# The small room moved to last but one, the last visit's tiles written one behind the other, weight buffers counted by use

## The chip, the core and the metric

One NeuronCore of a Trainium2 chip runs the whole kernel. The metric is the device time of one execution in microseconds, as the median of several runs. Engines: TensorE (PE, matmuls), VectorE (DVE), ScalarE (ACT), GpSimd (POOL, here the issuer of gathers and scatters) and SyncE (SP, which issues the weight loads).

## The reference

```python
# attention: q, k, v are (8, 8, 576, 64); mask 0 <= i - j < 128, bias -slope[h] * |i - j|
attn = softmax(where(mask, q @ k.T / 8 + bias, -1e9)) ; x = attn @ v        # -> (8, 576, 512)
# mixture of experts, 8 experts, w1 (8, 512, 1024), w2 (8, 1024, 512)
logits = x @ w_gate ; local = sigmoid(x @ w_local)
for s in range(576):                      # per batch
    e = argmax(logits[s]) if s == 0 or local[s] < 0.5 else prev_e ; prev_e = e
    out[s] = softmax(logits[s])[e] * (relu(x[s] @ w1[e]) @ w2[e])
```

All of it is in 32-bit floats.

## The kernel before, in words

The first part (attention and routing) fills about the first 280 us and is not touched. It leaves the tokens x in DRAM, grouped in blocks of 32, and tables of indices.

The second part is a list of **visits**, `PLAN`. A visit takes one expert's weights and a number of rows gathered for it. Three visits belong to fixed experts; the others go by rank, that is by how many tokens an expert got, and their sizes stand in `RANKS`. `ORDER_OF_ROOMS` puts them in order. By rows the rank visits run 512, 288, 384, 416, 256, 288, 384, 192, 256, 384, 224, 32. The text calls the 384-row visit near the end the long 384-row visit, and the one of 32 rows the small room.

A visit (`Fixed.run`) loops over eight hidden blocks f of 128. For each, 12 matmuls (`three`, once for each of 4 pieces of 128) make the hidden block h in PSUM; ScalarE writes its positive part hh (a reduced 32-bit type) and VectorE the rest hl; then `second(f - 1)` multiplies the block before with the second layer, three matmuls of 512 columns for each output tile of 128 rows. Every 32-bit product is made of three: high by high, high by low, low by high. A visit of 256 rows has two output tiles, ys[0] and ys[1]. `finish` scales an output tile, on ScalarE for even and on VectorE for odd tiles, and `scatter` sends it to the output through GpSimd.

**Weights** come through `Stream`, here W. A chunk (2 hidden blocks of one layer, "a" or "b", 512 KB) is loaded by SP into one of six raw buffers (`wraw`), then split: two casts on ScalarE for the high part, two subtractions on VectorE for the low part, into one of six `cut` buffers. `load` may run `RAWS` chunks ahead of the last one split, `fill` splits up to six chunks ahead of the first one in use. The small room's chunks are used raw, and its first-layer chunks lie in other buffers (`xT`).

**Rows** come through `Feed`. At each `tick` inside a visit it issues a gather (`take`, `gate`) on GpSimd and may `turn` a gathered tile: a transpose on VectorE into the single buffer xtr, a cast on ScalarE and a subtraction on VectorE, which write the high and low part of the tile qx that the h matmuls read. `turn` takes only tiles of visits up to `upto`, the next one; `Feed.finish` turns what is left at a visit's end.

The small room (`Mini`) comes last. Its first layer is put between the last h block and `second(7)` of the visit ahead of it, its hidden layer is turned by PE inside `second(7)`, and its second layer follows. After all visits the waiting scatters are issued, and a loop for tokens left over runs no times.

Of the kernel before, what the change touches and what calls it, by code (L numbers as in the profile page):

```python
# [16 lines left out]
P = 128  # L17
# [3 lines left out]
DM = 512  # L21
# [4 lines left out]
OWN = [2, 3, 4]  # L26

RANKS = [(512, 288), (384, 256), (384, 256), (384, 224), (416,), (288,), (192,), (32,)]
ORDER_OF_ROOMS = [0, 1, 2, 8, 3, 9, 4, 10, 5, 6, 7, 11]
NSB = 128  # L30
NFX = 32
SB = S // 32
# [48 lines left out]
def moe_attention(ctx, tc, qT, kT_d, vv, wg, wl, w1, w2, out):  # L81
# [65 lines left out]
    def run(g):  # L147
        for _ in g:
            pass
# [96 lines left out]
    class Stream:  # L246


        def __init__(self, order):
            self.order = order  # L250
            self.raw, self.cut, self.gone, self.n_raw, self.n_cut, self.first, self.depth = [], {}, set(), 0, 0, 0, 1

        def load(self):
            while self.n_raw < len(self.order) and self.n_raw < self.n_cut + RAWS:
                e, which, c, kind = self.order[self.n_raw]
                if kind and which == ("b" if kind == "also" else "a"):
                    if c % 2 == 0:
                        self.pair = tp.tile([P, 2, 2, DM], F32, name="xT")
                    t = self.pair[:, c % 2]
                else:  # L260
                    t = wr.tile([P, 2, DM], F32, name="wraw")
                self.raw.append(load_chunk(e() if callable(e) else e, which, c, t))
                self.n_raw += 1

        def fill(self):
            while self.n_cut < len(self.order) and self.n_cut < self.first + self.depth:
                self.load()
                if self.order[self.n_cut][3] == "only":
                    self.cut[self.n_cut] = self.raw.pop(0)
                    self.n_cut += 1  # L270
                else:
                    run(self.split(self.room(), now.act, nc.vector))
            self.load()

        def room(self):
            pool = vp if (self.n_cut - 1) % SPLITS < 4 else wp
            return pool.tile([P, 2, 2, DM], F32R, name="cut")

        def split(self, c, scalar, vector):
            raw = self.raw.pop(0)  # L280
            self.cut[self.n_cut] = c[:, 0], c[:, 1], raw
            self.n_cut += 1
            yield from split_chunk(raw, c, scalar, vector, self.n_cut - 1 if self is W else 0)

        def find(self, which):
            return min(i for i in self.cut if self.order[i][1] == which)

        def at(self, which):
            self.depth = min(self.depth + 1, SPLITS)
            self.fill()  # L290
            return self.cut[self.find(which)]

        def done(self, which):
            i = self.find(which)
            del self.cut[i]
            self.gone.add(i)
            while self.first in self.gone:
                self.first += 1
            self.fill()
# [717 lines left out]
    class Fixed:  # L1017
        def __init__(self, rows):
            self.rows = rows

        def run(self, W, tick, mini=None, ready=None):
            N = 32 * self.rows.blocks
            wins = windows(self.rows.blocks)
            n, rest = len(wins), wins[-1][1] % 4
            M = N - 32 * rest
            ys = [py.tile([P, DM], F32, name="y")[:, :P * r] for _, r in wins]
            xh, xl = self.rows.xh[:, :, :N], self.rows.xl[:, :, :N]
            hs, hx = {}, None

            def second(f, then=()):  # L1030
                hh, hl = hs.pop(f)
                vh, vl, raw = W.at("b")
                for t, (w, r) in enumerate(wins):
                    if r == 4:
                        sl = slice(32 * w, 32 * w + P)
                        three(ys[t], hh[:, sl], hl[:, sl], vh[:, f % 2], vl[:, f % 2], f == 0, f == 7)
                    elif f % 2:
                        rests(ys[t], lambda ff: hx[:, ff % 2], raw, (f - 1, f), r)
                    if t == n // 2 - 1:
                        tick()  # L1040
                        for g in then:
                            g()
                if f % 2:
                    W.done("b")

            for f in range(8):
                ah, al, _ = W.at("a")
                hp = ph_.tile([P, N], F32, name="h")
                for kc in range(4):
                    cs = slice(P * kc, P * kc + P)  # L1050
                    three(hp, ah[:, f % 2, cs], al[:, f % 2, cs], xh[:, kc], xl[:, kc], kc == 0, kc == 3)
                    if kc == 1:
# [12 lines left out]
                tick()  # L1065
                if f > 0:
                    second(f - 1)
                if rest and f % 2:
                    hx = hx_next
                tick()  # L1070
            if mini:
                ready()
                mini.first(W)
            second(7, [mini.turn] if mini else ())
            for t in range(n):
                c = self.rows.t0 + t
                finish(ys[t], self.rows.g[:, t:t + 1], self.rows.idx[2][:, c:c + 1], t % 2)
# [8 lines left out]
    class Mini(Fixed):  # L1086


        def first(self, W):
            raws = [W.at("a") if i == 0 else W.cut[W.find("a") + i] for i in range(4)]  # L1090
            hp = ph_.tile([P, 256], F32, name="h")
            for kc in range(4):
                for g in range(4):
# [190 lines left out]
    now.act = act  # L1284
    for i, v in enumerate(visits):
        if isinstance(v, Fixed):
            mini = visits[i + 1] if i + 2 == len(visits) else None
            v.run(W, lambda: feed.tick(i + 1), mini, lambda: feed.finish(i + 1))
            feed.finish(i + 1)
    assert table_done  # L1290

# [55 lines left out]
```

## Time and profile before

| | |
|---|---|
| median of 3 runs | 679.7 us (679.34 to 679.98) |
| the profiled execution | 678.48 us, of which its span is 676.8 us |
| PE busy | 656.5 us, 97% of the span |
| VectorE, ScalarE, GpSimd busy | 69%, 62%, 58% |
| mean granted TensorE clock | 0.995 |
| moved by DMA | 121 MB, mean 179 GB/s |

The span is the time from the first to the last instruction of the profiled execution. A busy share is a mean over the whole span; what bounds a stretch is read from the windows and the timeline of that stretch. Matmul durations overlap: a matmul counts as busy until its result is out, while the next one has already begun, so the start-to-start distance is what a matmul costs.

### The profile page before, as it was taken

To read this page: it belongs to the slowest core of one execution; us is meant where nothing else is said; L and a number is where in the kernel's file an instruction comes from. 1 tells how busy PE (TensorE), PEld (TensorE's weight loads), DVE (VectorE), ACT (ScalarE), POOL (GpSimd) and SP (SyncE) were. 2 spreads that over 40 slices of the span, in tenths; PEclk is the share of its full clock that TensorE was granted. 3 is DMA by queue.
4 is the path that set the end of the run, shared out by engine and by line. 5 is a ranking of instruction groups with operands and counts; after the bars stand their busy time and mean duration, and the time that the engine had idled before them with its cause. 6 is when DMAs were issued, how large, how long until landed. Compare 5 with 4: busy or idle time off the path is not lost. (4 is left out here: it accounts for less than half of the span.)

```text
span 676.8 us, 16362 instructions
## 1 busy us (share of the span) xinstructions
PE 656.5 (97%) x5485; PEld 528.0 (78%) x5485; DVE 466.0 (69%) x1637; ACT 418.1 (62%) x1217; POOL 392.6 (58%) x655
## 2 busy tenths in 40 slices
PE   8999999999999989999999999999999999999993
PEld 4667777677666678878888888988898898899882
DVE  6579889889888999975553657453776547774520
ACT  7999999999989644343442555353665536653421
POOL 7856656556687745877775476471577516761011
PEclk9999999999999999999999999999999999999998
DMA  9855754764813675554654268343846834774810
GB/s 287 275 143 156 240 170 144 218 194 152 255 68 110 196 265 179 164 148 148 228 189 135 82 225 281 96 133 128 287 152 205 281 99 143 241 224 152 274 54 34
DMA packets 60903, 121.09 MB, mean 179 GB/s; under 512 B 9260, under 2 KB 28204, under 8 KB 60816
## 3 DMA queue, kind: packets, MB, share of 16 engines
q1 hardware_dynamic: 51248, 100.12, 46.5%
q0 software_dynamic: 9136, 19.30, 9.3%
q8 instruction: 44, 0.72, 0.4%
q10 hardware_dynamic: 432, 0.59, 0.3%
q14 instruction: 43, 0.35, 0.2%
HBM read 101.03 MB, written 19.29 MB: 178 GB/s over the span
## 5 line engine op out<-in xcount | busy, mean ns | idle before, releaser
L182 POOL DMA_INDIRECT kr<-xd,xidx x141 | 155.3, 1101 | 55.3 <-issue 39.4
L1004 PE MATMUL h<-qx,cut 128*128 128x384 f32 (+6 forms) x440 | 142.4, 324 | 0.0
L1005 PE MATMUL h<-qx,cut 128*128 128x384 f32 (+6 forms) x440 | 140.8, 320 | 0.2 <-DVE qx L192 0.2
L1006 PE MATMUL h<-qx,cut 128*128 128x384 f32 (+6 forms) x440 | 140.9, 320 | 0.0
L243 DVE TENSOR_TENSOR cut<-wraw,cut 128x512 fp32r<-128x512 f32 x183 | 118.8, 687 | 30.0 <-ACT cut L241 28.6
L1056 ACT ACTIVATE hh<-h 128x384 fp32r<-128x384 f32 (+4 forms) x104 | 46.6, 448 | 132.9 <-PE h L1006 131.2
L167 POOL TENSOR_SCALAR cut<-cut,r 128x192 f32<-128x192 f32 (+2 forms) x256 | 99.6, 407 | 45.8 <-DVE r L167 16.2
L998 POOL DMA_INDIRECT out<-y,sidx x41 | 44.5, 1085 | 132.7 <-ACT y L1013 85.3
L1057 DVE SCALAR_TENSOR_TENSOR hl<-h,hh 128x256 fp32r<-128x256 f32 (+4 forms) x112 | 55.4, 496 | 88.4 <-ACT hh L1056 88.0
L1004 PE MATMUL y<-cut,hh 128*128 128x512 f32 x288 | 113.7, 395 | 0.8 <-ACT hh L167 0.8
L1006 PE MATMUL y<-cut,hl 128*128 128x512 f32 x288 | 113.1, 394 | 0.9 <-DVE hl L1057 0.9
L1005 PE MATMUL y<-cut,hh 128*128 128x512 f32 x288 | 113.3, 393 | 0.0
L167 ACT ACTIVATE cut<-scs,mn 128x192 f32<-128x192 f32 (+2 forms) x256 | 108.8, 429 | 5.3 <-DVE mn L167 5.0
L241 ACT CAST cut<-wraw 128x512 fp32r<-128x512 f32 x164 | 93.6, 618 | 24.6 <-PE y L1006 23.9
L1004 PEld LDWEIGHTS h<-qx,cut 128*128 128x128 f32 x440 | 83.0, 189 | 9.7 <-issue 3.9
L167 DVE CUSTOM_DVE_ANT_0 scs<-sc,bias 128x192 f32<-128x192 f32 (+2 forms) x288 | 83.1, 324 | 8.9 <-PE sc L167 5.6
L1005 PEld LDWEIGHTS h<-qx,cut 128*128 128x128 f32 x440 | 83.1, 189 | 5.7 <-DVE qx L192 0.7
L1006 PEld LDWEIGHTS h<-qx,cut 128*128 128x128 f32 x440 | 83.2, 189 | 2.7 <-issue 0.2
L167 PE MATMUL pt<-ident,cut 128*128 128x128 f32 x448 | 70.8, 282 | 0.6
L1006 PEld LDWEIGHTS y<-cut,hl 128*128 128x128 f32 x288 | 54.0, 188 | 13.5 <-DVE hl L1057 2.1
L167 PE MATMUL sc<-kr,qx 64*64 64x192 f32 (+2 forms) x1152 | 61.9, 319 | 1.2 <-DVE mn L167 1.2
L1004 PEld LDWEIGHTS y<-cut,hh 128*128 128x128 f32 x288 | 54.2, 188 | 10.7 <-ACT hh L167 1.8
(218 smaller groups left out, 1036.7 us busy)
## 6 DMA issues: line engine op xcount, KB each, us to landing
wraw<-w SPq DMA_DIRECT2D x100, 512.0 KB
xT<-w SPq DMA_DIRECT2D x20, 512.0 KB
kr<-kT SPq DMA_DIRECT2D x31, 288.0 KB
qx<-qT SPq DMA_DIRECT2D x30, 288.0 KB
cut<-v SPq DMA_DIRECT2D x8, 1024.0 KB
xd<-T SPq DMA_DIRECT2D x8, 768.0 KB
xd<-T SPq DMA_DIRECT2D x8, 384.0 KB
kr<-xd,xidx POOLq DMA_INDIRECT x141, 3.8
```

Source lines behind the costliest of these rows:

```text
L167: ins = getattr(self.engine, name)(*args, **kw)
L182: queued(nc.gpsimd.indirect_dma_start(out=r, out_offset=None, in_=src[0:n, :], in_offset=bass.IndirectOffsetOnAxis(ap=col, axis=0), bounds ...
L241: scalar.copy(c[:, 0, f], raw[:, f])
L243: (pool if 2 * n + f == POOL_CUT else vector).tensor_tensor(c[:, 1, f], raw[:, f], c[:, 0, f], ALU.subtract)
L998: queued(nc.gpsimd.indirect_dma_start(out=out.rearrange("t (a c) -> (t a) c", a=n), out_offset=bass.IndirectOffsetOnAxis(ap=col, axis=0), ...
L1004: nc.tensor.matmul(o, ah, bh, start=start, stop=False)
L1005: nc.tensor.matmul(o, ah, bl, start=False, stop=False)
L1006: nc.tensor.matmul(o, al, bh, start=False, stop=stop)
L1056: now.act.activation(hh, hp[:, :M], AF.Relu)
L1057: nc.vector.scalar_tensor_tensor(hl, hp[:, :M], 0.0, hh, ALU.max, ALU.subtract)
```

## The change

The rank visits now run 512, 288, 384, 416, 256, 288, 384, 192, 384, 224, 32, 256: the small room is last but one, and the 256-row visit that stood between the 192-row and the long 384-row one is last. The small room still shares its first layer and turn with the 224-row visit. In the last visit (`tail`) the second layer of blocks 5 to 7 is put off for output tile 1 and done as a whole behind tile 0; each tile is finished and scattered as soon as it is complete; scatters still waiting are issued ahead of the visit. `Stream` counts raw buffers by use: a raw buffer is live from its load until its chunk is split (or, for a chunk used raw, until it is done with), at most `RAWS` are live, chunks that lie in other buffers don't count but wait for their turn, and `fill` splits only what an earlier call has loaded, unless the chunk is asked for. The buffer for a split is chosen by a counter of splits.

```diff
-ORDER_OF_ROOMS = [0, 1, 2, 8, 3, 9, 4, 10, 5, 6, 7, 11]
+ORDER_OF_ROOMS = [0, 1, 2, 8, 3, 9, 4, 10, 6, 7, 11, 5]
...
+        def paired(self, i):
+            _, which, _, kind = self.order[i]
+            return kind in ("also", "only") and which == ("b" if kind == "also" else "a")
         def load(self):
-            while self.n_raw < len(self.order) and self.n_raw < self.n_cut + RAWS:
+            while self.n_raw < len(self.order) and self.live < RAWS:
                 e, which, c, kind = self.order[self.n_raw]
-                if kind and which == ("b" if kind == "also" else "a"):
+                if self.paired(self.n_raw):
+                    if self.n_raw > self.first + 2 * SPLITS:
+                        return
...
                     t = wr.tile([P, 2, DM], F32, name="wraw")
+                    self.live += 1
...
-        def fill(self):
-            while self.n_cut < len(self.order) and self.n_cut < self.first + self.depth:
+        def fill(self, upto=-1):
+            while self.n_cut <= upto or self.n_cut < min(self.first + self.depth, self.ready):
                 self.load()
...
             self.load()
+            self.ready = self.n_raw
         def room(self):
-            pool = vp if (self.n_cut - 1) % SPLITS < 4 else wp
-            return pool.tile([P, 2, 2, DM], F32R, name="cut")
+            self.n_room += 1
+            return (vp if (self.n_room - 1) % SPLITS < 4 else wp).tile([P, 2, 2, DM], F32R, name="cut")
         def split(self, c, scalar, vector):
             raw = self.raw.pop(0)
             self.cut[self.n_cut] = c[:, 0], c[:, 1], raw
+            if not self.paired(self.n_cut):
+                self.live -= 1
...
         def done(self, which):
             i = self.find(which)
             del self.cut[i]
             self.gone.add(i)
+            if self.order[i][3] in ("only", "raw") and not self.paired(i):
+                self.live -= 1
...
-        def run(self, W, tick, mini=None, ready=None):
+        def run(self, W, tick, mini=None, ready=None, tail=False):
...
-                if f > 0:
+                if tail and f == 6:
+                    vh, vl, _ = W.at("b")
+                    hh, hl = hs[5]
+                    three(ys[0], hh[:, 0:P], hl[:, 0:P], vh[:, 1], vl[:, 1], False, False)
+                elif f > 0 and not (tail and f == 7):
                     second(f - 1)
...
+            if tail:
+                assert n == 2 and not rest
+                chunks = [W.at("b"), W.at("b", 1)]
+                for t, fs in ((0, (6, 7)), (1, (5, 6, 7))):
+                    for f in fs:
+                        hh, hl = hs[f]
+                        sl, (vh, vl, _) = slice(P * t, P * t + P), chunks[f // 2 - 2]
+                        three(ys[t], hh[:, sl], hl[:, sl], vh[:, f % 2], vl[:, f % 2], False, f == 7)
+                    c = self.rows.t0 + t
+                    finish(ys[t], self.rows.g[:, t:t + 1], self.rows.idx[2][:, c:c + 1], t)
+                    scatter(*pending.pop())
...
-            mini = visits[i + 1] if i + 2 == len(visits) else None
-            v.run(W, lambda: feed.tick(i + 1), mini, lambda: feed.finish(i + 1))
+            mini = visits[i + 1] if i + 1 < len(visits) and isinstance(visits[i + 1], Mini) else None
+            if i + 1 == len(visits):
+                while pending:
+                    scatter(*pending.pop(0))
+            v.run(W, lambda: feed.tick(i + 1), mini, lambda: feed.finish(i + 1), i + 1 == len(visits))
```

What it moves, at the places of which the prediction speaks. First VectorE in the 192-row visit, before: y is an output tile of the visit ahead, xtr, kr and qx are a tile being turned for the next visit, cut a split chunk, hl the low part of a hidden block.

```order
L1011 TENSOR_SCALAR y_8816<-y_8499,gs_7991 128x512
L188 STREAM_TRANSPOSE xtr_8830<-kr_8513 128x512
L243 TENSOR_TENSOR cut_8807<-xT_8632,cut_8807 128x512 x2
L192 TENSOR_TENSOR qx_8829<-xtr_8830,qx_8829 128x4x128
L1057 SCALAR_TENSOR_TENSOR hl_8848<-h_8822,hh_8847 128x128
L188 STREAM_TRANSPOSE xtr_8853<-kr_8513 128x512
L192 TENSOR_TENSOR qx_8829<-xtr_8853,qx_8829 128x4x128
L1057 SCALAR_TENSOR_TENSOR hl_8883<-h_8863,hh_8882 128x128
```

The same place after the change:

```order
L1027 TENSOR_SCALAR y_8843<-y_8502,gs_8008 128x512
L188 STREAM_TRANSPOSE xtr_8857<-kr_8516 128x512
L243 TENSOR_TENSOR cut_8836<-xT_8563,cut_8836 128x512 x2
L192 TENSOR_TENSOR qx_8856<-xtr_8857,qx_8856 128x4x128
L1073 SCALAR_TENSOR_TENSOR hl_8875<-h_8849,hh_8874 128x128
L188 STREAM_TRANSPOSE xtr_8880<-kr_8516 128x512
L192 TENSOR_TENSOR qx_8856<-xtr_8880,qx_8856 128x4x128
L188 STREAM_TRANSPOSE xtr_8887<-kr_8516 128x512
L192 TENSOR_TENSOR qx_8856<-xtr_8887,qx_8856 128x4x128
L1073 SCALAR_TENSOR_TENSOR hl_8914<-h_8894,hh_8913 128x128
```

A third transpose and subtraction stand between the second tile and the low part of the second hidden block.

VectorE after the change, from the end of the 224-row visit (hl_9685 is its last hidden block, y_9740 its second output tile) to the first hidden blocks of the last visit (hl_9839 and hl_9856):

```order
L1073 SCALAR_TENSOR_TENSOR hl_9685<-h_9671,hh_9684 128x224
L243 TENSOR_TENSOR cut_9785<-wraw_9751,cut_9785 128x512 x2
L1027 TENSOR_SCALAR y_9740<-y_9458,gs_8947 128x512
L243 TENSOR_TENSOR cut_9798<-wraw_9758,cut_9798 128x512 x2
L188 STREAM_TRANSPOSE xtr_9806<-kr_9468 128x512
L192 TENSOR_TENSOR qx_9805<-xtr_9806,qx_9805 128x4x128
L188 STREAM_TRANSPOSE xtr_9810<-kr_9468 128x512
L192 TENSOR_TENSOR qx_9805<-xtr_9810,qx_9805 128x4x128
L1073 SCALAR_TENSOR_TENSOR hl_9839<-h_9825,hh_9838 128x256
L1073 SCALAR_TENSOR_TENSOR hl_9856<-h_9842,hh_9855 128x256
```

Both tiles of the last visit are turned there, behind the 224-row visit's output and a split; before, nothing followed that output.

GpSimd's queue at the end, before (y_9980 and y_9982 are the two tiles of the 224-row visit, y_10017 is the small room's):

```order
L998 DMA out<-y_9737,sidx_111 4608x512
L998 DMA out<-y_9739,sidx_111 4608x512
L998 DMA out<-y_9980,sidx_111 4608x512
L998 DMA out<-y_9982,sidx_111 4608x512
L998 DMA out<-y_10017,sidx_111 18432x128
```

And after the change, where y_9738, y_9740 and y_9803 are these three, y_10010 and y_10024 the tiles of the last visit:

```order
L1014 DMA out<-y_9455,sidx_111 4608x512
L182 DMA gs_9556<-gd_76,ridx_110 128x1
L1014 DMA out<-y_9738,sidx_111 4608x512
L1014 DMA out<-y_9740,sidx_111 4608x512
L1014 DMA out<-y_9803,sidx_111 18432x128
L1014 DMA out<-y_10010,sidx_111 4608x512
L1014 DMA out<-y_10024,sidx_111 4608x512
```

Two scatters follow the last visit instead of three that follow the small room and its neighbour.

## Rows read from the trace of the kernel before

**Rows 1.** The page: busy time, share of the span and instructions of PE, and the granted TensorE clock by fortieths of the span in tenths of full speed.

```profile
PE 656.5 (97%) x5485; PEld 528.0 (78%) x5485; DVE 466.0 (69%) x1637; ACT 418.1 (62%) x1217; POOL 392.6 (58%) x655
PEclk9999999999999999999999999999999999999998
```

**Rows 2.** The windows from 480 to 660 us, nine of 20 us: the line with their sum, busy us of each engine.

```profile
sum 180.00, PE 179.98 PEld 158.66 DVE 108.83 ACT 91.44 POOL 84.96; mean PE 20.00 PEld 17.63 DVE 12.09 ACT 10.16 POOL 9.44
```

**Rows 3.** The timeline of the end: start, duration in us, engine, line, operation, output and inputs, form, count; in brackets the idle time before and what ended it.

```profile
662.35 0.69 ACT L1013 ACTIVATE y<-y,gs 128x512 f32<-128x512 f32 x1 [0.48 <-PE y L1006]
...
662.83 0.40 PE L1006 MATMUL y<-cut,hl 128*128 128x512 f32 x1
...
663.26 0.75 DVE L1011 TENSOR_SCALAR y<-y,gs 128x512 f32<-128x512 f32 x1 [4.29 <-PE y L1006]
663.31 0.98 POOL L998 DMA_INDIRECT out<-y,sidx  x1 [14.54 <-ACT hh L1106]
...
663.35 1.96 PE L1084 MATMUL y<-wraw,hh 128*32 128x128 f32 x64
665.37 0.37 ACT L1013 ACTIVATE y<-y,gs 128x128 f32<-128x128 f32 x1 [2.08 <-PE y L1084]
667.23 0.98 POOL L998 DMA_INDIRECT out<-y,sidx  x1 [2.94 <-issue]
670.60 0.98 POOL L998 DMA_INDIRECT out<-y,sidx  x1 [2.39 <-issue]
```

**Rows 4.** The view of line 998, the scatters: under what their engine waited for, the landing of a scatter (us in total, times); then the time from issue to landing of all 41.

```profile
  DMA out<-y,sidx: 8.6, 3
...
DMA to landing us min/median/max: 2.8/4.0/6.7
```

**Rows 5.** The timeline of PE in the 256-row visit: its first matmul, the second and the 24th, then the first and the last of ten matmuls in a row of its second layer, then the first of the next visit.

```profile
582.89 0.39 PE L1004 MATMUL h<-qx,cut 128*128 128x256 f32 x1
583.11 0.28 PE L1005 MATMUL h<-qx,cut 128*128 128x256 f32 x1
...
585.75 0.28 PE L1006 MATMUL h<-qx,cut 128*128 128x256 f32 x1
...
603.25 0.39 PE L1006 MATMUL y<-cut,hl 128*128 128x512 f32 x1
...
605.31 0.39 PE L1006 MATMUL y<-cut,hl 128*128 128x512 f32 x1
605.53 0.33 PE L1004 MATMUL h<-qx,cut 128*128 128x384 f32 x1
```

**Rows 6.** The timeline of the 224-row visit: a split (casts on ScalarE, subtractions on VectorE), and two steps of the visit without one.

```profile
645.95 1.14 ACT L241 CAST cut<-wraw 128x512 fp32r<-128x512 f32 x2 [1.04 <-PE y L1006]
...
646.61 1.29 DVE L243 TENSOR_TENSOR cut<-wraw,cut 128x512 fp32r<-128x512 f32 x2 [1.27 <-ACT cut L241]
...
652.74 0.36 ACT L1056 ACTIVATE hh<-h 128x224 fp32r<-128x224 f32 x1 [2.37 <-PE h L1006]
...
655.46 0.36 ACT L1056 ACTIVATE hh<-h 128x224 fp32r<-128x224 f32 x1 [2.37 <-PE h L1006]
```

**Rows 7.** The last weight load's issue in SP's timeline, and the DMA view of 641 to 647 us: the busy share of the 16 DMA engines in tenths, by fortieths of the window (0.15 us each). The second burst, from the 24th digit on, belongs to the scatter at 643.32.

```profile
641.14 0.33 SPq L236 DMA_DIRECT2D wraw<-w  x1
...
DMA  5444322949337989597646000289992000000000
```

**Rows 8.** The timeline of GpSimd: the last gather ahead of a long idle stretch and the scatter that ends it; then two scatters of output tiles of the long 384-row visit.

```profile
543.66 0.99 POOL L182 DMA_INDIRECT kr<-xd,xidx  x1 [0.31 <-issue]
561.14 1.02 POOL L998 DMA_INDIRECT out<-y,sidx  x1 [16.48 <-ACT y L1013]
...
638.76 0.98 POOL L998 DMA_INDIRECT out<-y,sidx  x1 [23.52 <-ACT y L1013]
643.32 0.99 POOL L998 DMA_INDIRECT out<-y,sidx  x1 [3.58 <-DVE hl L1057]
```

**Rows 9.** The timeline of the 192-row visit: the turn of the second tile (transpose, cast, subtraction), the low part of the second hidden block, and the matmul that reads it.

```profile
564.61 0.70 DVE L188 STREAM_TRANSPOSE xtr<-kr 128x512 f32<-128x512 f32 x1
565.35 0.62 ACT L191 CAST qx<-xtr 128x512 fp32r<-128x512 f32 x1 [0.39 <-DVE xtr L188]
566.00 0.69 DVE L192 TENSOR_TENSOR qx<-xtr,qx 128x512 fp32r<-128x512 f32 x1 [0.69 <-ACT qx L191]
566.61 0.28 DVE L1057 SCALAR_TENSOR_TENSOR hl<-h,hh 128x128 fp32r<-128x128 f32 x1
566.95 0.49 PE L1006 MATMUL y<-cut,hl 128*128 128x512 f32 x1
```

**Rows 10.** Windows of the end: from and to, length, then for each engine busy us and instructions; behind them the mean granted clock, the DMA share and GB/s.

```profile
670.00:670.50 0.50, 0.00 (x0) 0.00 (x0) 0.00 (x0) 0.00 (x0) 0.00 (x0) 0.89 0.00 0
670.50:671.00 0.50, 0.00 (x0) 0.00 (x0) 0.00 (x0) 0.00 (x0) 0.40 (x1) 0.50 0.00 0
```

**Rows 11.** The timeline of PE at the start of the kernel: two groups of warm-up matmuls.

```profile
1.06 3.59 PE L167 MATMUL pk<-warm 128*128 128x512 f16 x8 [1.06 <-DVE warm L167]
...
9.35 1.47 PE L167 MATMUL pk<-warm 128*128 128x512 f16 x6
```

**Rows 12.** The waits of PE in the whole trace: us in total, times, longest.

```profile
PE h L1005 <- DVE qx L192: 0.2, 1, 0.2
```

More of the change, by code (lines that the diff above doesn't have):

```diff
@@ L250, in __init__ @@
             self.order = order
-            self.raw, self.cut, self.gone, self.n_raw, self.n_cut, self.first, self.depth = [], {}, set(), 0, 0, 0, 1
+            self.raw, self.cut, self.gone = [], {}, set()
+            self.n_raw = self.n_cut = self.n_room = self.first = self.live = self.ready = 0
+            self.depth = 1
+        def paired(self, i):
+            _, which, _, kind = self.order[i]
+            return kind in ("also", "only") and which == ("b" if kind == "also" else "a")
         def load(self):
-            while self.n_raw < len(self.order) and self.n_raw < self.n_cut + RAWS:
+            while self.n_raw < len(self.order) and self.live < RAWS:
                 e, which, c, kind = self.order[self.n_raw]
-                if kind and which == ("b" if kind == "also" else "a"):
+                if self.paired(self.n_raw):
+                    if self.n_raw > self.first + 2 * SPLITS:
+                        return
                     if c % 2 == 0:
@@ L261, in load @@
                     t = wr.tile([P, 2, DM], F32, name="wraw")
+                    self.live += 1
                 self.raw.append(load_chunk(e() if callable(e) else e, which, c, t))
                 self.n_raw += 1
-        def fill(self):
-            while self.n_cut < len(self.order) and self.n_cut < self.first + self.depth:
+        def fill(self, upto=-1):
+            while self.n_cut <= upto or self.n_cut < min(self.first + self.depth, self.ready):
                 self.load()
-                if self.order[self.n_cut][3] == "only":
+                if self.order[self.n_cut][3] in ("only", "raw"):
                     self.cut[self.n_cut] = self.raw.pop(0)
@@ L281, in split, with find, at @@
             self.cut[self.n_cut] = c[:, 0], c[:, 1], raw
+            if not self.paired(self.n_cut):
+                self.live -= 1
             self.n_cut += 1
             yield from split_chunk(raw, c, scalar, vector, self.n_cut - 1 if self is W else 0)
-        def find(self, which):
-            return min(i for i in self.cut if self.order[i][1] == which)
-        def at(self, which):
+        def find(self, which, nth=0):
+            return [i for i in range(self.first, len(self.order)) if self.order[i][1] == which and i not in self.gone][nth]
+        def at(self, which, nth=0):
             self.depth = min(self.depth + 1, SPLITS)
-            self.fill()
-            return self.cut[self.find(which)]
+            i = self.find(which, nth)
+            self.fill(i)
+            return self.cut[i]
         def done(self, which):
@@ L1070, in run @@
                 tick()
+            if tail:
[9 more added lines that the diff above has]
+                    scatter(*pending.pop())
+                W.done("b")
+                W.done("b")
+                return
             if mini:
@@ L1089, in first @@
         def first(self, W):
-            raws = [W.at("a") if i == 0 else W.cut[W.find("a") + i] for i in range(4)]
+            raws = [W.at("a", i) for i in range(4)]
             hp = ph_.tile([P, 256], F32, name="h")
```

## The prediction

> **What bounds the kernel now.** I began with the page [rows 1]: TensorE (PE) is busy 656.5 of 676.8 us, and its granted clock is at full speed in every slice but the last. Then the windows of the late visits [rows 2]: from 480 to 660 us PE is busy 179.98 of 180.00. So until the last matmul the time is a count of matmuls, and a wait put in front of PE there is added in full, since nothing later has room to take it back. Last the timeline of the end [rows 3]: the last matmul ends at 665.31, the span at 676.80. These 11.49 us belong to GpSimd's queue: three scatters at 663.31, 667.23 and 670.60, though their data is ready at 663.04, 664.01 and 665.74. Scatters wait for one another: the view of their line names the landing of an earlier one as what later ones waited for, and a landing takes 2.8 to 6.7 us [rows 4]. From the last scatter's start to the end it is 6.20 us.
>
> I keep the old trace's clock: the 256-row visit (582.89 to 605.53 [rows 5]) is cut out and put behind 665.31.
>
> **The move itself.** The visit took 22.64 us. Its 96 matmuls of 256 columns are 0.12 us apart (23 of them from 583.11 to 585.75), its 48 of 512 columns 0.229 (ten from 603.25 to 605.31 [rows 5]): 22.5 us. In its old place it also covered the turning of three tiles for the next visit; at the end it covers none. Term: -0.1 us. The small room's matmuls, its wait for the copied hidden layer and its scatter stay.
>
> **Weight buffers.** The order of loads, splits and matmuls is unchanged until the 192-row visit, so I cost the new counting up to there at nothing. In the 224-row visit five chunks of the last visit are now split: ten casts and ten subtractions of some 0.6 us each, in gaps of ScalarE of 2.37 us per step of 2.72 [rows 6]; VectorE's gaps are alike. The small room's four second-layer chunks hold four of the six raw buffers until its matmuls end, so these loads go in turn through the other two, each issued when a split frees its buffer. A pair of subtractions ends 1.95 us behind its first cast (645.95 to 647.90 [rows 6]), so two steps less 1.95 leave 3.5 us from that to the split that wants the new chunk. A load alone, issued at 641.14, has stopped moving data by some 644.3, 3.1 us later [rows 7]. It fits with 0.4 us to spare, and a late cast has 1.2 us more before the next activation waits behind it. Cost: nothing. If the cover fails it comes back at the last visit's start, below.
>
> **Gathers.** The long 384-row visit now follows the 192-row one, so its 12 row gathers and 3 gates run where 8 and 2 ran, before 560 us: five more at 1.3 us, in an idle stretch of GpSimd of 16.48 us [rows 8]. Nothing.
>
> **The third tile in the 192-row visit.** Before, this visit turned two tiles for its successor; now three. In VectorE's order the third transpose and subtraction stand ahead of the low part hl of the second hidden block. On the old clock the second subtraction ends at 566.69; then a transpose of 0.70, a cast of 0.62 and a subtraction of 0.69, one behind the other because they share one buffer, with 0.03 to 0.06 us between them, end at 568.83 [rows 9]. hl starts near 568.75 instead of 566.61. The matmul that reads it started at 566.95, right behind hl's end at 566.89, and would start at 569.09. Term: +2.1 us. Bounds: 0 if it is absorbed, 2.5 if the cast waits a little for ScalarE.
>
> **The start of the last visit.** Its tiles are turned only after the small room's code, since the feed turns tiles for a visit that is next and no further. In VectorE's order: the 224-row visit's second output tile, a split of two subtractions, then transpose, subtraction, transpose, subtraction. The split's casts stand behind the small room's copy on ScalarE, and their target buffer is free when the 224-row visit's last matmul ends, 662.83 + 0.40 = 663.23 [rows 3]: casts from 663.28, the split done 1.95 later, 665.23. A turn is transpose, cast, subtraction: 2.08 us from start to end (564.61 to 566.69 [rows 9]). So the first ends at 667.3. The second starts behind it, has its cast done at 668.7 and ends at 669.4. PE is free at about 665.1, since a matmul's modelled tail overlaps the next by some 0.2 us (0.28 busy, 0.12 apart [rows 5]). Its first two matmuls need both casts; the third needs the low parts, and 21 follow closely. Delay: 669.4 - 665.1 - 0.24 of work = 4.1 us. Bounds: 2.9 if the split were done before (the first transpose then starts at 664.0); 5.2 if a load is 1.1 us late.
>
> **The tail.** Tile 0 of the last visit now ends nine matmuls ahead, 9 x 0.229 = 2.06 us. With E the end of the last matmul: its ScalarE output takes 0.05 + 0.69 us and the scatter follows 0.27 later, as 663.04 to 663.31 [rows 3]: E - 1.05. The second scatter waits for that landing: 3.92 us between the first pair of rows 3, 3.37 between the next, and 4.56 where loads run beside them [rows 8]. I take 3.92, a pair of full-width tiles as here: E + 2.87. Then 6.20 us, and 0.5 more (estimated: a full tile's data moves longer than the small room's): E + 9.57, against E + 11.49. With 3.37 it is E + 9.0. Between them the term is -2.1 us. Bounds: -1.3 (4.56), and -4.0 if the scatter waits only for its data at E + 0.8.
>
> **Sum.** -0.1 + 2.1 + 4.1 - 2.1 = +4.0 us on the profiled execution: 678.48 becomes 682.5. The median of the runs, 679.7, lies 1.2 above that execution, so I forecast **683.7 us**, 0.6% slower. About 0.2%, 1.4 us, is what a measurement here can tell from no change.
>
> **Rivals.**
>
> *The clock falls in the gap* (0.13). PE would stand 3.6 us, issue two matmuls, and stand 0.5 more. After the last matmul the granted clock stayed at 1.00 until about 670.4, when PE had stood 5.1 us, then read 0.50 [rows 10]: from 2.4 to 1.2 GHz. For it: the gap is not much shorter. Against: it is shorter. Price: the eight warm-up matmuls that open the kernel took 3.59 us; six later ones took 1.47, so eight at full speed would take 1.47 + 2 x 0.229 = 1.93 [rows 11, 5]. A slow restart of that size costs 1.7 us: 685.4.
> The Trainium skill, "TensorE: Matmul & The Clock Gate", section "HAM oscillation — how this bites in real kernels", has a stream of matmuls that is broken by waits throttled again in the wait and each group started cold. By that rule the time would be the 685.4 of this rival. The trace agrees only that the clock falls after work stops; no gap inside this kernel is long enough to show more.
>
> *The third tile is absorbed* (0.12): 683.7 - 2.1 = 681.6. For: the 256-row visit covered three turns and lost 0.1 us [rows 5]. Against: there hidden blocks lay between the tiles; here none does.
>
> *Every turn is covered, the tail alone counts* (0.05). Place: the tile turns ahead of PE. In the whole trace PE waited once on a turned tile, 0.2 us [rows 12]. If the last visit's turn ended before PE is through with the small room, the 4.1 and 2.1 us would go and the 2.1 of the tail stay gained: 677.5, faster. It decides by whether the last turn's end, which I put at 669.4, comes before 665.1; the split and both turns would have to start 4.3 us earlier than the order of instructions lets them.
>
> *The edit does less than it says* (0.02): the tail's pair of scatters 4.56 us apart and a load 1.1 us late: 683.7 + 0.8 + 1.1 = 685.6.
>
> **Numbers.** The forecast has the remaining chance, 0.68. The range runs from the absorbed tile with a little more tail (681.2) to a slow restart with a late scatter (686.0); outside lie the third rival and several bounds taken together. Slower by over 0.2%, above 681.1: 0.68 + 0.13 + 0.12 + 0.02, less 0.06 for both stalls coming out short: 0.89. Faster: 0.05. The same: 0.06.
>
> **What would show it.** Right: PE waits of some 3.6 and 0.5 us for the turned tile (qx) at the last visit's start and about 2 us for hl in the 192-row visit; the last two scatters 3.4 to 3.9 us apart; the end 9 to 9.6 us behind the last matmul; a granted clock of 1.00 throughout. Wrong: no PE wait above 1 us behind the small room, which fells the 4.1; an unbroken 192-row visit, which fells the 2.1; a tail of 11 us or of 7.5; matmuls of 256 columns 0.2 us apart in the last visit, which is the first rival.

## The result and the profile after

| | before | after |
|---|---|---|
| median of the runs | 679.64 us (679.34 to 679.98) | 686.43 us (684.16 to 689.12) |
| profiled execution, its span | 678.48, 676.8 us | 684.16, 682.5 us |
| same pair again, another chip | 679.21 us | 687.39 us (684.89 to 687.87) |

On four of the chips that the later runs came to every kernel stalled, the one before too, and took 740 to 800 us; these two pairs are from calm ones. The change makes the kernel slower: ratio 1.0101 [1.0064, 1.0138], and 1.0102 [1.0083, 1.0120] in the second pair. I had forecast the direction, and 683.7 us. The median lies 2.7 us above that and 0.4 above the top of the range. The profiled execution lies 1.7 us above its forecast of 682.5.

The page of after, against [rows 1]: PE is busy 1.8 us longer, the span is 5.7 us longer, and the clock is down in two slices at the end and not one.

```profile
span 682.5 us, 16366 instructions
...
PE 658.3 (96%) x5485; PEld 529.1 (78%) x5485; DVE 466.8 (68%) x1638; ACT 418.1 (61%) x1217; POOL 393.1 (58%) x655
...
PEclk9999999999999999999999999999999999999988
```

The waits of PE for the tiles and hidden blocks of the visits, against the single 0.2 us of [rows 12] (us in total, times, longest):

```profile
PE h L1020 <- ACT qx L191: 3.4, 1, 3.4
PE y L1020 <- ACT hh L1072: 1.7, 1, 1.7
PE h L1021 <- DVE qx L192: 0.4, 2, 0.2
```

The second row is the 192-row visit. Its timeline, against [rows 9]:

```profile
567.16 0.71 DVE L188 STREAM_TRANSPOSE xtr<-kr 128x512 f32<-128x512 f32 x1
...
567.91 0.62 ACT L191 CAST qx<-xtr 128x512 fp32r<-128x512 f32 x1 [1.50 <-DVE xtr L188]
568.43 0.27 ACT L1072 ACTIVATE hh<-h 128x128 fp32r<-128x128 f32 x1
568.56 0.69 DVE L192 TENSOR_TENSOR qx<-xtr,qx 128x512 fp32r<-128x512 f32 x1 [0.68 <-ACT qx L191]
...
568.76 0.50 PE L1020 MATMUL y<-cut,hh 128*128 128x512 f32 x1 [1.73 <-ACT hh L1072]
569.17 0.29 DVE L1073 SCALAR_TENSOR_TENSOR hl<-h,hh 128x128 fp32r<-128x128 f32 x1
...
569.51 0.51 PE L1022 MATMUL y<-cut,hl 128*128 128x512 f32 x1
```

The third tile's transpose, cast and subtraction stand where I put them, ahead of hl. What I had not seen is that the third cast also stands ahead of hh on ScalarE, so PE stops one matmul group earlier; the delay is the same. The first row of the waits is the start of the last visit:

```profile
643.37 1.95 PE L1118 MATMUL y<-wraw,hh 128*32 128x128 f32 x64
...
645.15 0.70 DVE L188 STREAM_TRANSPOSE xtr<-kr 128x512 f32<-128x512 f32 x1
...
648.01 0.62 ACT L191 CAST qx<-xtr 128x512 fp32r<-128x512 f32 x1 [1.50 <-DVE xtr L188]
648.66 0.69 DVE L192 TENSOR_TENSOR qx<-xtr,qx 128x512 fp32r<-128x512 f32 x1 [0.68 <-ACT qx L191]
...
648.68 0.51 PE L1020 MATMUL h<-qx,cut 128*128 128x256 f32 x2 [3.36 <-ACT qx L191]
...
649.41 0.58 PE L1021 MATMUL h<-qx,cut 128*128 128x256 f32 x1 [0.22 <-DVE qx L192]
```

Then what I had left out: the windows behind it (the granted clock is the third figure from the end). PE works at half the clock from 649.3 to about 652.8; the fall itself comes 0.7 us behind the end of the wait.

```profile
649.00:650.00 1.00, 0.78 (x5) 0.60 (x4) 0.35 (x1) 0.00 (x0) 0.98 (x1) 0.67 0.00 0
650.00:651.00 1.00, 1.00 (x6) 1.00 (x6) 0.00 (x0) 0.00 (x0) 0.23 (x1) 0.50 0.23 90
651.00:652.00 1.00, 1.00 (x7) 1.00 (x6) 0.00 (x0) 0.00 (x0) 0.00 (x0) 0.50 0.29 109
652.00:653.00 1.00, 1.00 (x7) 1.00 (x7) 0.37 (x1) 0.38 (x1) 0.36 (x1) 0.62 0.00 0
653.00:654.00 1.00, 1.00 (x9) 0.95 (x8) 0.06 (x1) 0.14 (x1) 0.62 (x1) 1.00 0.00 0
```

And the end, against [rows 3]. The last matmul ends at E = 673.49; the first scatter starts at E - 1.08, the second 3.48 us behind it, the span ends at E + 9.0.

```profile
672.41 0.98 POOL L1014 DMA_INDIRECT out<-y,sidx  x1 [18.79 <-ACTq L1333]
...
673.10 0.39 PE L1022 MATMUL y<-cut,hl 128*128 128x512 f32 x1
673.52 0.75 DVE L1027 TENSOR_SCALAR y<-y,gs 128x512 f32<-128x512 f32 x1 [2.68 <-PE y L1022]
...
675.89 0.98 POOL L1014 DMA_INDIRECT out<-y,sidx  x1 [2.51 <-issue]
```

### The profile page after: what moved, and what is told of

The parts are those of the page before. It is cut to its first block, busy times and chain, and to the rows that moved or that the text cites. A ratio compares the mean times of both kernels' runs of the same rounds, so it can differ in the third digit from the quotient of the medians.

```text
span 682.5 us, 16366 instructions
## 1 busy us (share of the span) xinstructions
PE 658.3 (96%) x5485; PEld 529.1 (78%) x5485; DVE 466.8 (68%) x1638; ACT 418.1 (61%) x1217; POOL 393.1 (58%) x655
```

## The experiments

The theory: every wait is where the prediction has it, and the excess is the clock, which falls in the gaps that the waits make. The rival: a further wait, elsewhere. The runs down to the one without the written-out end came to chips that stalled, and from them only stretches without a stall are used; the later ones, on calm chips, are compared by their medians too.

**The changed kernel again** (no edit).

> The changed kernel once more, unaltered, to see how far its executions differ. Theory (the clock falls in the 3.6 us gap at the last visit's start, and not equally long in every execution): the times spread again over some 684 to 689 us, and a longer time goes with a lower mean granted clock and with a longer stretch at half speed around the gap. Rival (the excess over the sum of the prediction is a wait, not the clock): the profile shows the same clock as the first one, whatever the time, and the extra us stand as an idle stretch of PE elsewhere.

> The changed kernel unaltered, a third time, beside the kernel before: in the first repetition both took some 780 us, with stalls of PE all over the second part that the first profiles don't have, so the difference of the two was lost in them. Theory (clock and gaps, as in the prediction): about 4 to 7 us above the kernel before, spread over several us; where an execution is longer than the first profile (682.5 us span), its clock is lower. Rival (the change costs nothing where runs are not alike): the two are equal within 1 us.

> The changed kernel unaltered, for the times alone, should this chip not stall as the last ones did. Theory: 4 to 7 us above the kernel before; executions fall into such as lost 3.4 us of clock-time at half speed and such as lost 6.8 us or more, some 1.7 us apart. Rival: stalls as on the last chips, and no difference to the kernel before that can be told.

Medians of 777.9, 757.5 and 761.4 us, ratios to before of 1.0021 [0.9968, 1.0073], 0.9987 [0.9929, 1.0044] and 1.0004 [0.9938, 1.0071]: the expected times were missed, nothing can be told from these. The local facts repeat: in the three profiles PE waits 3.2, 3.7 and 3.4 us for qx at the last visit's start, the clock falls there each time, and the end comes 8.98 us behind the last matmul.

**Work in the gap.**

```diff
             feed.finish(i + 1)
+            if isinstance(v, Mini):
+                pw = ptk.tile([P, 512], F32, name="pk")
+                for _ in range(14):
+                    pin(nc.tensor.matmul(pw, identb, identb.unsqueeze(1).broadcast_to([P, 4, P]), start=True, stop=True))
```

> Fourteen matmuls of 128x512 that nobody reads (16-bit inputs that lie ready, so they wait for nothing) are put behind the small room's second layer: 14 x 0.229 = 3.2 us of work in a gap of 3.4 us; order and waits of all else stay. Theory (the clock's fall in the gap costs what my sum lacks): granted clock 1.00 through 645 to 655 us, matmuls of 256 columns 0.12 us apart right behind the gap, median about 683.7 us, which is the prediction's own sum, with a spread under 1 us. Rival (the excess is a wait elsewhere): the clock stays up but the median stays near 686.4.

> The fourteen idle matmuls in the gap once more. Theory (the slow restart behind the gap costs 1.5 to 1.9 us, and what the other executions lose beyond the first profile is lost at the same place): about 683.7 us, spread under 1 us, 1.5 to 3 us below the changed kernel on the same chip. Rival (what the other executions lose has another place): faster than the changed kernel by 1.5 to 1.9 us only, with the same spread of several us.

Medians 775.3 and 759.1 us, 0.9900 [0.9842, 0.9957] and 0.9968 [0.9911, 1.0026]. In both profiles the clock stays at 1.00 through the gap. From the small room's first second-layer matmul to the last matmul's end: 28.8 and 29.0 us, against 30.1 in the first profile of the changed kernel, 29.8, 31.5 and 30.9 in the three above, and 30.1 in the kernel with the third tile later, below.

**The last visit's turns earlier.** The two tiles are turned at the ends of hidden blocks 5 and 6 of the 224-row visit (the small room's x gets its own buffer for that).

```diff
                 tick()
+                if mini and f in (5, 6):
+                    ahead()
...
-            v.run(W, lambda: feed.tick(i + 1), mini, lambda: feed.finish(i + 1), i + 1 == len(visits))
+            v.run(W, lambda: feed.tick(i + 1), mini, lambda: feed.finish(i + 1), i + 1 == len(visits), lambda: feed.turn(i + 2, 0))
```

> The last visit's two tiles are turned inside the 224-row visit, at the ends of its hidden blocks 5 and 6, in place of behind the small room. Theory (the wait for the two turned tiles, 4.1 us, and the slow restart that it brings are both gone): PE does not stand for more than 0.5 us behind the small room, granted clock 1.00 there, and 686.4 less 4.1 less what the clock cost, 686.4 - 683.7 = 2.7: about 679.6 us, spread under 1 us. Rival (the turns move, but the split of the weights that stood ahead of them in the two engines' queues is what ends last): PE still stands for 2 us or more, 682 us or above.

Median 771.4 us, 0.9933 [0.9883, 0.9982]. No wait at the last visit's start, clock 1.00 there, the stretch 24.6 us.

**The third tile later.**

```diff
-                if x[0] <= upto and self.clock >= x[2] + lag:
+                if x[0] <= upto and self.clock >= x[2] + lag and not (lag and x[1] == 2 and PLAN[x[0]] == SPACED and self.clock < self.last + 6):
+                    self.last = self.clock
```

> The third tile that the 192-row visit turns for its successor is put off by six ticks, so that hidden blocks lie between it and the second. All else, the gap at the last visit's start too, stays. Theory (the third turn in a row delays the low part of a hidden block by 2.1 us): PE's wait of 1.7 us there is gone, and the median is 2.1 us below that of the changed kernel, 684.3, with as wide a spread. Rival (the wait is made up later or only moves to the third tile's new place): PE waits there instead, and the median stays at 686.4.

Median 774.7 us, 0.9898 [0.9837, 0.9960]; the gap and the fall at the last visit's start are there (3.3 us; 30.1 us). In the 192-row visit PE waits for nothing, and the visit takes 22.59 us where it took 23.70 in the changed kernel's first profile: the local part came as expected. The median, on a chip that stalled, cannot be held against the 684.3 expected.

**Both mends.**

> The two mends together: the last visit's two tiles turned inside the 224-row visit (4.1 us and the slow restart), the 192-row visit's third tile put off (2.1 us). Theory: -0.1 of the move and -2.1 to -2.5 of the tail are left, so 2 to 2.5 us below the kernel before: 677.3 us beside 679.7. Rival (the gain of the tail is lost elsewhere, or the mends push other work late): no better than the kernel before.

> The two mends together once more, for the time. Theory: without stalls 2 to 2.5 us below the kernel before (677.3 beside 679.7); with them 10 us below it again, which would be more than the terms of the prediction explain. Rival: no better than the kernel before.

Medians 753.3 and 753.1 us, 0.9814 [0.9721, 0.9907] and 0.9950 [0.9888, 1.0012]. The first is below the kernel before, the second's interval takes in 1, and on these chips I cannot say by what they gained.

**Half the gap** (one turn early, one left: `f in (5, 5)` in place of `(5, 6)`).

> Only tile 0 of the last visit is turned inside the 224-row visit; tile 1 stays behind the small room. Judged by the stretch from the small room's second layer (its first matmul) to the last matmul, which was 30.1, 29.8, 31.5 and 30.1 us in four profiles with both turns there, 28.8 and 29.0 with matmuls in the gap, 24.6 twice with both turns early. One turn less: PE waits some 1.3 us for the cast and 0.4 for the subtraction. Theory (the clock falls only after a longer stand): no stretch at half speed, 24.6 + 1.3 + 0.4 = 26.3 us. Rival (any stand of a microsecond brings the clock down): half speed behind it, 27.4 to 28.8 us.

The stretch took 26.65 us, the theory's 26.3 within 0.4. PE stood 1.29 and 0.22 us:

```profile
725.78 2.00 PE L1120 MATMUL y<-wraw,hh 128*32 128x128 f32 x64
...
729.08 0.50 PE L1020 MATMUL h<-qx,cut 128*128 128x256 f32 x2 [1.29 <-ACT qx L191]
```

The clock read 1.00 in the windows around and behind it, so the theory stands, by one profile:

```profile
727.00:732.00 5.00, 3.48 (x48) 3.01 (x43) 2.17 (x5) 1.37 (x3) 0.58 (x1) 1.00 0.65 231
732.00:737.00 5.00, 5.00 (x33) 4.48 (x33) 2.47 (x5) 1.85 (x5) 1.46 (x2) 1.00 0.15 55
```

**Without the written-out end** (both mends, and `tail` False in the last visit).

> Both mends (as in the kernel with the two of them), but the last visit without its own end: its two output tiles are made block by block as in any other visit. With E the end of the last matmul, tile 0 then ends three matmuls ahead of E and not nine. Theory (the tail's gain is the lead of the first scatter, since the second follows it at 3.48 us and the end 6.6 us later, as in all profiles of the changed kernel): the first scatter at E + 0.1, the end at E + 10.2 in place of E + 9.0; of the 2.5 us gained on the kernel before, 1.2 come from the written-out end, 1.3 from two scatters in place of three. Rival (the second scatter waits for its own data only, or three scatters cost nothing): E + 7.5 or E + 11.5.

With E = 754.30 the first scatter starts at E + 0.3, the second 4.26 us later and not 3.48, the end is E + 11.1:

```profile
754.62 0.98 POOL L1014 DMA_INDIRECT out<-y,sidx  x1 [13.54 <-ACTq L1339]
...
758.88 0.98 POOL L1014 DMA_INDIRECT out<-y,sidx  x1 [3.28 <-issue]
```

So of the tail's 2.5 us the written-out end brings 2.1 (11.1 to 9.0), by the lead of the first scatter and a shorter step to the second; two scatters in place of three bring the 0.4 that is left to 11.49. I had expected 1.2 and 1.3: a miss in the division. This is one profile: all seventeen that have the written-out end show the step of 3.48 to 3.50, but why the step is longer here is not shown.

**The kernel before, for its stalls.**

> The kernel before the change, profiled on one of these chips. On them the changed kernel was 3 to 6 us below it by the medians of all executions, where the first runs had it 6.8 above. Theory (other engines stand while GpSimd issues a train of gathers, and the change has moved a train): PE's stands without a cause in the profile lie where GpSimd issues gathers one behind the other, in the second part, and they cost this kernel some 8 to 10 us more than the changed one, at the visits that the change has moved. Rival (the stalls come at any place): PE's stands lie apart from GpSimd's trains.

This run came to a calm chip: 678.84 us, span 677.1, PE's waits as in [rows 12], no stalls. It tests nothing of that theory. It shows that the two profiles of before agree within 0.3 us.

**The four kernels on one calm chip.**

> The changed kernel, beside the kernel before and three relatives, for the times on a chip that doesn't stall (the last run took 678.8 us for the kernel before). Theory: 684 to 689 us, median near 686.4; the executions differ by how long the clock stayed at half speed behind the gap at the last visit's start: mean clock .993 goes with 684.2, .991 with 686, .989 with 688 or 689. Rival (the excess over the prediction's sum is no matter of the clock): times differ at one mean clock.

> The fourteen idle matmuls in the gap: only the clock is meant to differ from the changed kernel. Theory (the clock's fall is all that the prediction missed): 682.5 to 683.7 us, spread under 1 us, clock .995, so 2.7 to 3.9 us below the changed kernel's median. By the stretches of the profiles from the stalling chips (28.9 against 29.8 to 31.5 us) at least 0.9. Rival: the same median and spread as the changed kernel.

> Both turns of the last visit inside the 224-row visit. Theory: the wait of 4.1 us and the slow restart both go: 679.5 us, spread under 1 us; the same as the kernel before within 0.5 us, since the 2.1 of the third tile and the 2.1 to 2.5 of the tail cancel. Rival: above 681.

> The two mends together. Theory: 2.1 us below the one with the early turns alone, 677.3 us, 2 to 2.5 below the kernel before. Rival (the third tile's turn, put off, makes PE wait at its new place): no better than the one with the early turns alone.

| | median us (range) | ratio to before | first 384-row matmul to E | E to the end |
|---|---|---|---|---|
| before (profile above) | 679.21 (678.30 to 679.90) | | 409.99 | 11.49 |
| changed, first profile | 686.43 | 1.0101 [1.0064, 1.0138] | 417.78 | 9.01 |
| changed, again | 687.39 (684.89 to 687.87) | 1.0102 [1.0083, 1.0120] | 421.38 | 8.98 |
| work in the gap | 684.93 (683.54 to 686.80) | 1.0088 [1.0072, 1.0103] | 416.33 | 8.99 |
| early turns | 680.27 (679.25 to 681.69) | 1.0013 [1.0004, 1.0022] | 414.21 | 8.99 |
| both mends | 678.67 (676.49 to 679.49) | 0.9993 [0.9984, 1.0002] | 410.84 | 9.00 |

The executions of the changed kernel, both pairs together, fall into three by their mean clock: at 0.993 and 0.994 they took 684.2 to 685.0 us, at 0.991 686.1 to 687.4, at 0.989 687.8 to 689.1. A longer time goes with a lower clock, as the theory of c_again has it. Its profile is one of the long ones (span 686.1), and its waits show more than the theory:

```profile
PE h L1020 <- ACT qx L191: 3.4, 1, 3.4
PE y L1020 <- ACT hh L1072: 1.7, 1, 1.7
PE tr L1138 <- ACT hl L1133: 1.2, 1, 1.2
```

The third wait is new. The windows of this profile, in the 192-row visit and at the last visit's start:

```profile
566.00:567.00 1.00, 1.00 (x10) 0.86 (x8) 0.56 (x1) 0.41 (x1) 0.89 (x1) 1.00 0.21 66
...
568.00:569.00 1.00, 0.24 (x1) 0.24 (x2) 0.44 (x1) 1.00 (x3) 0.70 (x2) 0.94 0.06 21
...
570.00:571.00 1.00, 1.00 (x5) 0.54 (x6) 0.85 (x3) 0.14 (x2) 0.69 (x2) 0.50 0.11 37
...
650.00:651.00 1.00, 0.00 (x0) 0.00 (x0) 0.62 (x1) 0.35 (x1) 0.00 (x0) 0.90 0.52 209
...
652.00:653.00 1.00, 1.00 (x5) 0.95 (x5) 0.00 (x0) 0.00 (x0) 0.94 (x1) 0.50 0.00 0
...
656.00:657.00 1.00, 1.00 (x7) 1.00 (x6) 0.00 (x0) 0.00 (x0) 0.44 (x1) 0.50 0.00 0
```

Here the clock fell behind the 1.7 us stand of the 192-row visit too, and at the last visit it stayed down until about 657.6. So not all of what the clock costs lies at the last visit's start. The new wait is told by the timeline:

```profile
640.13 1.14 ACT L241 CAST cut<-wraw 128x512 fp32r<-128x512 f32 x2 [1.85 <-DMA wraw<-w]
...
643.28 1.14 ACT L241 CAST cut<-wraw 128x512 fp32r<-128x512 f32 x2 [1.75 <-DMA wraw<-w]
...
644.32 0.38 ACT L1133 ACTIVATE hl<-h 128x256 f32<-128x256 f32 x1
...
644.75 0.44 PE L1138 MATMUL tr<-ident,hl 128*128 128x128 f32 x2 [1.17 <-ACT hl L1133]
```

The DMA view of 624 to 646 us, the weight loads (count, KB each, median us from issue to landing; of these seven the trace has the landing of one alone, issued at 635.57):

```profile
wraw<-w SPq DMA_DIRECT2D x7, 512.0 KB, 4.5
```

And the waits of ScalarE for them:

```profile
ACT cut L241 <- DMA wraw<-w: 8.7, 5, 2.0
```

A cast that waits for weights stands ahead of the small room's hidden layer, and PE waits for that: a further wait, as the rival had it. Before, casts waited 1.6 us for weights in the whole trace. In the changed kernel's first profile they wait 7.3, and PE still doesn't:

```profile
640.23 1.14 ACT L241 CAST cut<-wraw 128x512 fp32r<-128x512 f32 x2 [1.21 <-DMA wraw<-w]
```

c_warm's median came 1.2 us above the theory's upper end, with a spread of 3.3 us: the gap's clock is not all. Its interval also overlaps that of the changed kernel beside it, so what the clock in the gap costs is read from the profiles and not from these two medians. Its two shortest executions (683.54 and 683.96) have a mean clock of 0.997, the longer ones, 684.9 to 686.8, 0.994 or 0.995. In its profile the clock is at 1.00 throughout. c_early lies 0.8 above its theory; its profile shows the fall in the 192-row visit, and the new wait with 0.5 us. c_both is 1.6 us below c_early and not 2.1, and its median is 1.4 us above its theory.

**Late weights put behind.** The cast of the fifth split is made to stand behind the copy of the small room's hidden layer.

```diff
-            scalar.copy(c[:, 0, f], raw[:, f])
+            ins = scalar.copy(c[:, 0, f], raw[:, f])
+            if n == len(order) - 4:
+                tc.add_manual_dep(ins.ins, W.behind.ins.name, ...)
...
-            now.act.copy(self.hT, pt)
+            W.behind = now.act.copy(self.hT, pt)
```

> The kernel with both mends, and the fifth of the last visit's splits (a cast that waits for its weights' landing, up to 1.8 us, ahead of the small room's hidden layer on ScalarE) put behind the copy of that hidden layer. In the profile of the changed kernel on a calm chip PE stood 1.2 us for that layer, and the kernel with both mends took 676.5 us in its profile but 678.7 in the median. Theory (late weights in that place are what the other executions lose): 676.5 to 677.3 us, 1.4 to 2 us below the kernel with both mends on the same chip. Rival (they lose it elsewhere): the same median as that kernel.

> The kernel with both mends beside it, unaltered: 678.7 us again on a calm chip, and a second profile, in which PE stands some 1 to 2 us for the small room's hidden layer if the execution is a long one.

677.66 us, 0.9979 [0.9970, 0.9988], and 678.11 us, 0.9982 [0.9972, 0.9993]: some 0.4 us apart with overlapping intervals, so the rival stands. The second profile of both mends (678.24 us, span 676.5) shows no new wait either; it is of middling length, so the wait that I expected of a long one was not put to the test. Most of what it is longer than the first by lies in the part that no kernel here changes. The first matmul of the first 384-row visit, in the two profiles of both mends:

```profile
254.96 0.34 PE L1020 MATMUL h<-qx,cut 128*128 128x384 f32 x1
```

```profile
256.44 0.34 PE L1020 MATMUL h<-qx,cut 128*128 128x384 f32 x1
```

The kernel with the late cast put behind has the lowest median of all, 1.5 us below the kernel before on its chip, but it is not told apart from both mends.

## Why the prediction was wrong

**The waits and the tail were right.** c_warm's profile has no fall of the clock, and it is the prediction's own sum made visible: from the first 384-row matmul to E it takes 416.33 - 409.99 = 6.3 us more than before (my terms: -0.1 + 2.1 + 4.1 = 6.1), and with its tail of -2.5 it ends 3.8 us later (forecast 4.0). The 192-row visit takes 23.70 us in the changed kernel (561.77 to 585.47) and took 21.56: +2.1, as said. What is left of the 6.3, 4.2, is the move and the last visit's start, 4.0 in the sum. The tail is -2.5 and not -2.1, since the two scatters stand 3.48 us apart and I took 3.92; the estimated 0.5 us for the data of a full tile, which no row showed, measured 0.4 (6.57 us from the last scatter's start to the end, against 6.20). That is the lower of my two values, E + 9.0.

**The step that failed is the first rival's weight**: "Against: it is shorter." I took the 5.1 us for which the clock outlasted the last matmul [rows 10] as a measure of what PE can stand for, gave the fall 0.13, and put nothing for it into the sum. That was one reading of a figure that varies: in the changed kernel's first profile the clock falls at 676.65, 3.2 us behind the last matmul (673.49), and over all twenty profiles the distance is 2.7 to 5.3 us, so 5.1 was near its top.

```profile
676.00:676.50 0.50, 0.00 (x0) 0.00 (x0) 0.00 (x0) 0.00 (x0) 0.50 (x1) 1.00 0.00 0
676.50:677.00 0.50, 0.00 (x0) 0.00 (x0) 0.00 (x0) 0.00 (x0) 0.38 (x1) 0.65 0.00 0
```

In all six profiles in which PE stood 3.2 to 3.7 us behind the small room, the clock fell. The price by [rows 11] was sound for one fall: 1.7 us, where the last visit, from its first matmul to E, takes 24.81 us in the first profile and 23.36 in c_warm, so 1.45. But it was no upper bound: c_again's takes 25.79, so 2.4. That the median lies only 0.4 us above the range is luck: its top held a late scatter, which did not come. The Trainium skill, "TensorE: Matmul & The Clock Gate", section "HAM oscillation — how this bites in real kernels", says that a stream broken by waits is throttled in the wait; the runs agree with it for waits of 3.2 to 3.7 us, though in two of the six the clock fell just behind the wait.

**A second fall had no place in the sum.** The third tile's stand of 1.7 us brought the clock down in c_again and c_early and not in the first profile and c_warm. Where it did, the 192-row visit takes 24.94 us (561.78 to 586.72) in place of 23.70: 1.2 us more.

**"Cost: nothing" for the weight loads held in some executions only.** I let a chunk have 3.5 us and read 3.1 from one load's bursts [rows 7]. In c_again a cast is released 4.3 to 4.8 us behind the issue of the load that it waits for, by way of example 4.5 (635.57 to 640.05). With the 1.95 us of a split and two buffers in turn that is (4.5 + 1.95) / 2 = 3.2 us for each chunk against the 2.72 us of a step [rows 6]; the five casts of c_again that waited start 3.3 us apart (630.11 to 643.28). Each is later than the one before, and the fifth cost PE 1.2 us. In the first profile the last four of these casts are released 3.7 to 3.9 us behind the issue, the five start 2.9 us apart (628.66 to 640.23), and PE does not wait: the cover failed there too, but the time in reserve behind it sufficed. I had put this at 1.1 us in the last rival, at 0.02, and at another place.

**The account.** First profile: +4.2 +2.1 +1.45 -2.5 = 5.3 against 5.31 by the table (417.78 + 9.01 - 421.48). c_again: +4.2 +2.1 +1.2 +1.2 +2.4 -2.5 = 8.6 against 8.88. The medians, 6.8 and 8.2 us above before, lie between or near these. Which of the losses came together in the other executions is not shown; they have a mean clock but no profile.

**Open.** Both mends leave 0.9 us of the 6.1 (410.84 against 409.99), 0.7 of it in the 192-row visit, which takes 22.27 us, in gaps of 0.2 us and less between its hidden blocks. Seven profiles of the changed kernel and its relatives reach the first 384-row visit at 254.96 to 256.50 us, both of before at 255.32: whether the change costs something there is not settled. That late weights cost PE something is shown by two profiles on calm chips, 1.2 us in c_again and 0.5 in c_early; taking the cast out of the way gained some 0.4 us, which is not told apart from nothing. Why a load took longer in c_again than in the first profile was not found.

## What to carry to other kernels

A gap that you put in front of a full TensorE has two prices, the wait and the clock behind it; give the second a term of its own unless rows of the same length, and more than one, show the clock standing. A cover with 0.4 us to spare is no cover: read the landings of several transfers and not the bursts of one, and when a chain of them is slower than the step it feeds, count how late the last one is. Turn the next visit's tiles wherever hidden blocks lie between them, even two visits ahead.

## What the runs showed of the hardware

Stands of PE of 3.2 to 3.7 us behind the small room brought the clock down in six profiles of six. The stand of 1.7 us in the 192-row visit did in two of four on calm chips, and in five of seven on the others a fall came within 3.7 us of its start. A stand of 1.3 us (half) and one of 1.2 (c_again) were followed by none. Behind the small room PE then worked at half speed for some 3.4 us in three of the six profiles and 6.8 in the other three.

On the chips that stalled, other engines stood while GpSimd issued indirect transfers one behind the other. In the first such profile ScalarE stands 16.9 us for "remote", and 11 issues, 1.3 us apart, begin in that time; the view of waits names this releaser for none of the longer waits of the changed kernel's first profile.

ScalarE's timeline, then GpSimd's (the first and the last of the 11):

```profile
445.31 0.61 ACT L241 CAST cut<-xT 128x512 fp32r<-128x512 f32 x1
462.85 0.38 ACT L1072 ACTIVATE hh<-h 128x256 fp32r<-128x256 f32 x1 [16.93 <-remote]
```

```profile
446.08 1.01 POOL L182 DMA_INDIRECT kr<-xd,xidx  x1 [0.30 <-issue]
...
459.20 1.00 POOL L182 DMA_INDIRECT kr<-xd,xidx  x1 [0.30 <-issue]
```

Trains of gathers 1.3 us apart stand in the calm profile too (442.78 to 459.62 us in the first of the changed kernel), so they are not the cause by themselves; what differs between the chips was not found. One chip stalled in one run and was calm in a later one.
